# One order for TensorE with PSUM banks taken from a pool, and two feed-forward units moved behind attention

## The chip, the core and the metric

The kernel runs on one core of a Trainium2 chip. The metric is the device time of one execution in microseconds (us): the median of three runs was 1132.9 before the change (1132.64 to 1134.83). A difference of about 0.2% (2.3 us) is what a measurement of this kernel can tell from none.

The core has these engines: TensorE (PE, matrix products; its weight loads are shown as PEld), VectorE (DVE), ScalarE (ACT), GpSimd (POOL) and SyncE (SP, which here only issues DMAs). Each takes its instructions from a queue of its own, in order. Products land in PSUM, eight banks of 128 x 512 words; operands lie in SBUF. An engine waits for another by semaphores.

## The reference

For x of 2048 rows and 640 columns, attention a(x) with 32 heads of 20 columns and a gated feed-forward b(x) with 1728 features are mixed row by row by a gate. Attention works on four segments of 512 rows: within a segment it is causal softmax attention, and from the second segment on a memory M, z of the segments before it is read too.

```
def _A_ref(x, wq, wk, wv, wo, beta):          # H = 32, Dh = 20, N = 4, L = 512
    for s in range(N):
        logits = einsum("bhqd,bhkd->bhqk", qs, ks) * scale + mask
        a_dot = einsum("bhqk,bhkd->bhqd", softmax(logits), vs)
        a_mem = einsum(phi(qs), M) / (einsum(phi(qs), z) + 1e-6)
        o = g * a_mem + (1.0 - g) * a_dot      # g = sigmoid(beta), per head
        M, z = M + phi(ks)^T vs, z + sum(phi(ks))
    return o @ wo
def _B_ref(x, w1, w3, w2):
    return (silu(x @ w1) * (x @ w3)) @ w2
g = sigmoid((x * gate_w).sum(-1))
return g * a + (1 - g) * b
```

## The kernel before

**Numbers.** A product of two 32-bit operands is made of three passes over operands that are split into a high and a low part (`PASSES`): high by high, high by low, low by high. The split is an ACT copy into the rounded form and a subtraction on DVE or POOL (`split`, L487). `split_psum` (L518) does the same for operands of x and for the row maxima, but first copies the high part into a PSUM bank with ACT, so that the DVE subtraction has one input in SBUF and one in PSUM. It is called 10 times for x (segments 2 and 3, L687) and 32 times for the row maxima (L1210).

**Dense work.** The segments are taken in pairs, A = (0, 1) and B = (2, 3). For each pair: q, k and v projections (`proj`), the memory, then the feed-forward in five groups of features, `GROUPS` (L1417): [13, 0, 1], [2, 3, 4], [5, 6, 7], [8, 9, 10], [11, 12]. For most features a `unit` (L1023) makes the gate and up products of both segments with seven half products instead of eight: 54 matmuls of 128 x 512, tile names g, w, x (also under g) and u, four weight tiles from DRAM, and some twenty steps on DVE, ACT and POOL. `ffn_down` (L1127, tile f) multiplies a group by w2 and adds each of the five blocks of a segment into `acc` with one DVE step (L1149). `normalize(c)` (L1322) scales the attention output of segment c by the row sums (tile rr), adds the memory part (transposes, tile gt) and splits it; `oproj(c)` (L1390) multiplies by wo (tile op, 75 matmuls for each of two segments at the end), and `finish` writes the result.

**Attention.** It runs through 32 quads of four heads. A quad has two visits (`VISITS`, L1358), a big one of eight fills and a small one of three. An s fill makes scores in two banks, with four or two matmuls each, of which DVE takes the row maxima (L1200, sixteen per quad, each a pass over the bank and a short accumulator read). `max_rows` (L1206) brings the maxima back as two more rows of q by a DMA (qk<-mr). A t fill makes transposed scores less the maxima in two banks; ACT takes the exponential into P (L1232), POOL clears what the mask forbids (L1241). The o fill (`pv_quad`, L1246) multiplies P by v with a column of ones, which gives the row sums too, and stores the result to DRAM (od<-oq, L1258). After the last quad of a segment `o_sums` (L1265) loads its row sums back (rs<-od, L1267, on SP's queue), `o_scale` (L1274) takes their reciprocal on DVE, splits it in three (L1281 to L1286) and writes it out to be rR (L1288). `load_out` loads the attention output back, with the memory part on POOL's queue (L1316) and the rest on SP's (L1303, L1305).

**The order.** The program is traced once, with dense jobs fed between visits at a pace that spreads them (`segs`, each with an end in heads, and the main loop from L1582), and with a `tail` (L1514) behind the last visit. `braid(a, b, every)` puts a step of b behind each `every` steps of a. During tracing `bank_tile` (L496) gives each PSUM tile one of eight banks, by a small model of when banks come free; the choice is then fixed. At the end `Model.arrange` (L231) makes the final order of every queue by simulating all engines: `length` (L78) gives each instruction a time; each instruction has a due time, worked back from PE's order; every engine other than PE takes the ready instruction that is due first; PE takes, among the next `AHEAD` = 48 groups (up to three dense matmuls, or one fill), the first that is ready and whose banks are free:

```
for g in range(first, min(first + AHEAD, len(groups))):
    if g not in gone and not wants[g] and earlier[g] <= gone and all(map(enabled, groups[g])):
        run = groups[g][::-1]
```

The order found is then tied down with dependencies. On the chip each engine follows it, whatever the real times are.

Of the kernel before, what the change touches and what calls it, by code (L numbers as in the profile page):

```python
# [19 lines left out]
P = 128  # L20
# [12 lines left out]
LANES, SPARE, SOON = 8, 3, 5000  # L33
# [7 lines left out]
ON_CHIP = {}  # L41
ENGINES = {mybir.EngineType.PE: "PE", mybir.EngineType.DVE: "DVE", mybir.EngineType.Activation: "ACT",
# [6 lines left out]
class Tags:  # L49
# [28 lines left out]
def length(i, e, outs, ins):  # L78
# [9 lines left out]
    if e == "PE":  # L88
# [6 lines left out]
        else:  # L95
            d = 0.453 * n * (2 if wide and n < 500 else 1) + (20 if wide else 0)
        return d, max(d, 232) + 165
    if e == "DVE":
        d = 155 + 1.04 * n
        if "Transpose" in kind:  # L100
            d = 200
        elif "Reciprocal" in kind:
            d = 150 + 6.2 * n
        elif len(outs) > 1:
            d += 97
    elif e == "ACT":
        d = 170 + 0.85 * n
    else:
        d = 100 + (2.3 if len(ins) > 1 else 0.98) * n
# [3 lines left out]
class Model:  # L113


    def __init__(self, tc, nc, tags):
# [4 lines left out]
        self.end, self.free, self.gaps = [], {e: 0.0 for e in GAP}, {e: [] for e in GAP}  # L121
        self.lane, self.flown, self.way = [], {"HW": [], "SW": []}, 0.0

    def box(self, ap):
# [6 lines left out]
        if tag[0] == "b" and tag[1:].isdigit():  # L131
# [22 lines left out]
    def add(self, i):  # L154
# [8 lines left out]
        for write, args in ((False, ins), (True, outs)):  # L163
            for a in args:
# [4 lines left out]
                bank = not dram and box[1:] == (P, 0, 4 * L) and self.tags[name][0][0] == "b"  # L169
# [60 lines left out]

    def arrange(self):  # L231
# [11 lines left out]
        due, t = [math.inf] * n, 0.0  # L243
        for k in range(n):
            if eng[k] == "PE":
                due[k] = t
                t += dur[k]
        after, before = [[] for _ in range(n)], {}
        for x, (g, c) in tiles.items():
# [5 lines left out]
            if y is not None:  # L255
                before[users[x][0]] = users[y][0]
        for k in reversed(range(n)):
            if eng[k] != "PE":
                for s in succ[k] + after[k]:
                    due[k] = min(due[k], due[s] - HOP[eng[s]] - land[k])  # L260
                if k in before:
                    due[k] = min(due[k], due[before[k]])
        for k in range(n):
            if due[k] == math.inf:
                due[k] = t
        left = [len(p) for p in pred]
        ready = {e: [] for e in GAP}
        groups, group, earlier, tail = [], {}, [], {}
        for k in range(n):
# [12 lines left out]
            tail[x] = len(groups) - 1  # L282
        groups = [ks for _, ks in groups]
        wants = [sum(len(pred[k]) for k in ks) for ks in groups]
        gone, first, run = set(), 0, []
        busy = {e: 0.0 for e in GAP}
# [1384 lines left out]
```

## Time and profile before

| what | value |
|---|---|
| median of three runs | 1132.9 us |
| the profiled execution | 1130.5 us, span 1128.7 us |
| PE, DVE, POOL, ACT busy | 1096.7, 732.3, 510.2, 410.6 us |
| mean granted clock of PE | 0.991 of full |
| DMA | 222.8 MB moved, mean 197 GB/s |
| first and last matmul of attention starts | 129.9 us, 1054.1 us |

A row of the timeline has start and length in us, then engine, line, operation, output <- inputs, shapes and a count of merged instructions; in brackets the idle time before it and what ended it. A row of the waits has the total, the times and the longest. A matmul's length is its latency, and consecutive ones overlap, so its rate is read from starts. PE's busy time counts matmuls that stand within a run.

### The profile page before, as it was taken

To read this page: it belongs to the slowest core of one execution; us is meant where nothing else is said; L and a number is where in the kernel's file an instruction comes from. 1 tells how busy PE (TensorE), PEld (TensorE's weight loads), DVE (VectorE), ACT (ScalarE), POOL (GpSimd) and SP (SyncE) were. 2 spreads that over 40 slices of the span, in tenths; PEclk is the share of its full clock that TensorE was granted. 3 is DMA by queue.
4 is the path that set the end of the run, shared out by engine and by line. 5 is a ranking of instruction groups with operands and counts; after the bars stand their busy time and mean duration, and the time that the engine had idled before them with its cause. 6 is when DMAs were issued, how large, how long until landed. Compare 5 with 4: busy or idle time off the path is not lost.

```text
span 1128.7 us, 18096 instructions
## 1 busy us (share of the span) xinstructions
PE 1096.7 (97%) x6152; PEld 828.8 (73%) x6152; DVE 732.3 (65%) x1905; ACT 410.6 (36%) x825; POOL 510.2 (45%) x633
## 2 busy tenths in 40 slices
PE   9999999999999999899999998999999999999978
PEld 6988877767767777568877676767777667767756
DVE  6022568786886878884445577776776776775474
ACT  6244235232322323353344443334423423425110
POOL 6085334794875868646473213322322332322400
PEclk9999999999999999999999999999999999999979
DMA  8389745574755657976478776576756656634832
GB/s 300 133 257 313 266 147 163 194 251 151 228 186 175 214 170 225 292 221 190 154 246 265 246 228 186 155 230 206 193 142 181 184 137 179 182 113 154 258 99 84
DMA packets 120475, 222.81 MB, mean 197 GB/s; under 512 B 13280, under 2 KB 32896, under 8 KB 120384
## 3 DMA queue, kind: packets, MB, share of 16 engines
q1 hardware_dynamic: 95920, 175.91, 46.7%
q0 software_dynamic: 20432, 38.68, 15.1%
q10 hardware_dynamic: 4032, 7.08, 1.7%
q8 instruction: 49, 0.80, 0.3%
q14 instruction: 42, 0.34, 0.1%
HBM read 125.92 MB, written 94.78 MB: 196 GB/s over the span
## 4 chain that ended last, share of the span: by engine, by line
PE 51%; DMA 2%; DVE 2%; ACT 1%; issue 1%; SPq 0%; DVEq 0%; ACTq 0%
PE g L1033 8%; PE f L1141 7%; PE op L1404 6%; PE o L1252 4%; PE q L698 3%; PE u L1033 3%; PE s L1193 3%; PE v L828 3%; PE k L698 3%; PE t L1228 3%; PE w L1033 1%; PE g L698 1%; DMA od<-oq 1%; PE u L698 1%; PE nd L796 1%; ACT P L1232 1%
## 5 line engine op out<-in xcount | busy, mean ns | idle before, releaser
L1200 DVE CUSTOM_DVE_ANT_0 junk<-s,mask 128x256 bf16<-128x256 f32 (+3 forms) x512 | 250.8, 490 | 105.9 <-PE s L1193 69.4
L1232 ACT ACTIVATE P<-t 128x512 f32<-128x512 f32 x320 | 167.7, 605 | 160.2 <-PE t L1228 157.8
L1141 PE MATMUL f<-ht,W 128*128 128x512 f32 x820 | 203.6, 401 | 4.9 <-ACT ht L488 1.9
L1141 PEld LDWEIGHTS f<-ht,W 128*128 128x128 f32 x820 | 151.8, 189 | 45.5 <-POOL ht L489 2.5
L1241 POOL TENSOR_SCALAR_AFFINE_SELECT P<-P 128x512 f32<-128x512 f32 (+1 forms) x160 | 91.5, 581 | 157.0 <-ACT P L1232 154.5
L618 POOL TENSOR_TENSOR W<-wr,W 128x640 fp32r<-128x640 f32 (+3 forms) x92 | 139.9, 1521 | 6.9
L1170 POOL DMA_DIRECT2D qk<-qkd x128 | 83.0, 650 | 105.5 <-PE s L1193 53.6
L617 POOL CAST W<-wr 128x640 fp32r<-128x640 f32 (+3 forms) x92 | 71.5, 777 | 129.2 <-PE v L828 43.4
L489 POOL TENSOR_TENSOR ht<-fu,ht 128x512 fp32r<-128x512 f32 x44 | 58.6, 1337 | 73.6 <-ACT ht L488 73.6
L1193 PE MATMUL s<-qk 60*128 60x256 f32 (+3 forms) x512 | 79.9, 355 | 0.7 <-DVE oq L1256 0.3
L1404 PE MATMUL op<-N,W 128*128 128x512 f32 x300 | 77.9, 409 | 1.4 <-issue 0.6
L1252 PE MATMUL o<-P,vg 128*32 128x512 f32 (+3 forms) x1024 | 75.6, 435 | 1.7 <-DVE fw L1095 0.9
L1149 DVE TENSOR_TENSOR acc<-f,acc 128x512 f32<-128x512 f32 x80 | 54.5, 689 | 31.2 <-PE f L1141 30.5
L1033 PE MATMUL u<-T,W 128*128 128x512 f32 x264 | 70.3, 399 | 3.2 <-DVE fv L1075 3.2
L1033 PE MATMUL g<-XB,W 128*128 128x512 f32 x264 | 72.1, 401 | 0.1
L1228 PE MATMUL t<-qk 62*128 62x256 f32 (+3 forms) x512 | 69.1, 336 | 1.3 <-ACT P L1232 0.7
L1193 PEld LDWEIGHTS s<-qk 60*128 60x128 f32 x512 | 43.8, 186 | 34.9 <-issue 21.2
L1404 PEld LDWEIGHTS op<-N,W 128*128 128x128 f32 x300 | 55.7, 193 | 17.2 <-issue 1.9
L1228 PEld LDWEIGHTS t<-qk 62*128 62x128 f32 x512 | 46.3, 187 | 23.8 <-issue 11.4
L1252 PEld LDWEIGHTS o<-P,vg 128*32 128x32 f32 x1024 | 30.4, 109 | 45.1 <-issue 34.4
L1033 PEld LDWEIGHTS u<-T,W 128*128 128x128 f32 x264 | 48.7, 188 | 16.4 <-DVE fv L1075 4.5
L1033 PEld LDWEIGHTS g<-XB,W 128*128 128x128 f32 x264 | 48.3, 188 | 12.9 <-issue 0.4
(194 smaller groups left out, 1836.7 us busy)
## 6 DMA issues: line engine op xcount, KB each, us to landing
qk<-qkd POOLq DMA_DIRECT2D x128, 240.0 KB, 4.7
wr<-in_w_dram SPq DMA_DIRECT2D x40, 320.0 KB
qkd<-qs SPq DMA_DIRECT2D x20, 512.0 KB
qkd<-ks SPq DMA_DIRECT2D x20, 512.0 KB
wd_down<-W SPq DMA_DIRECT2D x14, 640.0 KB
W<-wd_down SPq DMA_DIRECT2D x14, 640.0 KB
od<-oq SPq DMA_DIRECT2D x32, 256.0 KB
wd_all<-W SPq DMA_DIRECT2D x11, 640.0 KB
```

The source lines that it names most:

```text
L618: nc.gpsimd.tensor_sub(w[:, 1, :n], src, w[:, 0, :n].bitcast(F32))
L698: nc.tensor.matmul(ps, w[:, a, kb * P:(kb + 1) * P], xs(c, b, kb), start=n == 0, stop=n == 14)
L1033: nc.tensor.matmul(ps, w[:, a, col + i * P:col + (i + 1) * P], x(i, b), start=start and t == 0, stop=stop and t == 3 * n - 1, skip_group_c ...
L1141: nc.tensor.matmul(ps[:, :n1 - n0], w, h, start=n == 0, stop=n == len(ms) - 1)
L1170: here(nc.gpsimd.dma_start(t[64 * i:64 * i + RH], qkd[c][RH * (h + i):RH * (h + i + 1)]))
L1193: nc.tensor.matmul(ps[i][:, o:o + w], q[:, qb * P:(qb + 1) * P], key[:, :w], start=n == 0, stop=n == len(todo) - 1, skip_group_check=True)
L1200: r = nc.vector.tensor_tensor_reduce(out=junk[:, :w], in0=ps[i][:, o:o + w], in1=mask[:, L - w:], scale=1.0, scalar=-3.0e38, op0=ALU.add, ...
L1228: nc.tensor.matmul(ps[i][:, o:o + L - kb * P], key[:, kb * P:(kb + 1) * P], q[:, kb * P:], start=n == 0, stop=n == len(todo) - 1, skip_gro ...
L1232: last["exp"] = nc.scalar.activation(pt[:, i], ps[i], AF.Exp, scale=SCALE)
L1241: nc.gpsimd.affine_select(d, d, pattern=pattern, base=0, channel_multiplier=-1, compare_op=ALU.is_ge, fill=0.0)
L1252: nc.tensor.matmul(ps[32 * i:32 * i + 32, kb * P:], heads[2 * p + i]["v"][:, kb], pt[:, i % 2, o:o + L - kb * P], start=kb == 0, stop=kb = ...
L1404: nc.tensor.matmul(ps, ws[kb][:, b, fb * P:(fb + 1) * P], n_tile(c, kb)[:, a], start=n == 0, stop=n == 14)
```

## The change

Four things.

**The order** is made by a new function `schedule`, which `arrange` calls for each of two settings of (stay, pause, spare, near) and takes the order that ends first by its own reckoning. PE's choice (`choose`) is new: within a visit it takes the next fill of the same visit that can go, and if one can go within `stay` (300 or 150 ns) it waits for it; else it takes the group that is first in turn, or waits for it if it can go within `pause` (150 ns); only then others. Leaving dense work for a visit is reckoned at `TURN` = 93 ns more, matmuls after a window of 3413 ns that was more than half idle at double length. A freed buffer, and a result for another engine, count 50 ns later than before.

**Banks.** All PSUM tiles are one tag of eight in the model; a tile gets a bank when the simulated PE reaches it, of those free the one whose last tile stands latest in program order, provided that tiles in a bank stay in program order (`seq`). A group out of turn must leave `RESERVE` = 4 banks that can still serve the earliest tile without one. The plan found is written in the string `BANKS`, one digit per tile, and the program is traced with it. `split_psum` no longer uses a bank or the ACT copy into it; its subtraction reads the high part from SBUF.

**Costs.** In `length` the 97 ns extra for a DVE instruction with two outputs (the row maxima) go; short 32-bit matmuls cost 3.4 instead of 2 times the base; POOL's affine select has its own cost; what waits for the load of the row sums (rs) is let go `LATE` = 2000 ns after its reckoned landing, so the DVE steps on the row sums are placed later.

**The tail.** The units of the last group of pair B, features 11 and 12, leave the last dense segment of the attention stage and stand behind the last visit, with the loads of segment 2's attention output between their steps; then the last `ffn_down` with the loads for segment 3 and `normalize(2)` between its steps; then the output projections as before.

```diff
-LANES, SPARE, SOON = 8, 3, 5000
+LANES, WINDOW, TURN, LATE, HANG = 8, 3413, 93, 2000, 0
+CHOICES, ROUNDS = ((300, 150, 3, 5000), (150, 150, 3, 5000)), 1
+RESERVE = 4
...
+BANKS = (
+    "0012310202020202020202001121101121101121101121101102120303032145671556742351572517175213461515643272"
...
-    def tile(self, shape, dt, name, tag=None, bufs=None):
+    def tile(self, shape, dt, name, tag=None, bufs=None, real=None):
         kw = {}
         if tag is not None:
-            kw["tag"] = tag
+            kw["tag"] = real or tag
         if bufs is not None:
-            kw["bufs"] = bufs
...
-            d = 0.453 * n * (2 if wide and n < 500 else 1) + (20 if wide else 0)
+            d = 0.453 * n * (3.4 if wide and n < 200 else 1) + (20 if wide else 0)
...
-        elif len(outs) > 1:
-            d += 97
...
-        d = 100 + (2.3 if len(ins) > 1 else 0.98) * n
+        d = 208 + 0.84 * n if "Affine" in kind else 100 + (2.3 if len(ins) > 1 else 1.0) * n
...
+    def schedule(self, plan, due, stay, pause, spare, near):
...
+        def fits(g):
+            new = [tiles[x][1] for k in groups[g] for x in set(of.get(k, ())) if users[x][0] == k and x not in held and tiles[x][0] == "bank"]
+            if not new:
+                return True
+            m, chosen = low(), set()
+            for i in new:
+                b = max((b for b in range(8) if not taken[b] and b not in chosen and seq[b] < i), key=lambda b: seq[b], default=None)
+                if b is None:
+                    return False
+                chosen.add(b)
+            if m in new:
+                return True
+            return sum(seq[b] < m and b not in chosen for b in range(8)) >= (1 if g == first else RESERVE)
+
+        def can(g):
+            return g not in gone and not wants[g] and earlier[g] <= gone and fits(g) and all(map(enabled, groups[g]))
+
+        def choose():
+
+            nonlocal first, of_late
+            while first in gone:
+                first += 1
+            if first == len(groups):
+                return None
+            if visit[of_late]:
+                for g in range(of_late + 1, len(groups)):
+                    if visit[g] != visit[of_late]:
+                        break
+                    if g not in gone:
+                        if can(g):
+                            return g
+                        if soon(g) <= now + stay:
+                            return None
+            if can(first):
+                return first
+            if soon(first) <= now + pause:
+                return None
+            for g in range(first + 1, min(first + AHEAD, len(groups))):
+                if can(g):
+                    return g
+            return None
...
+        def enabled(k):
+            if lane[k]:
+                some = LANES - (spare if due[k] + slip - now > near else 0)
+                if len(flown[lane[k]]) >= some and not landed.issuperset(flown[lane[k]][-LANES:1 - some or None]):
+                    return False
+            return all(x in held or eng[k] == "PE" and k != users[x][0] and group.get(users[x][0]) == group[k] or k == users[x][0] and (any(not taken[b] and seq[b] < tiles[x][1] for b in range(8)) if tiles[x][0] == "bank" else
+                       tiles[x][1] == given[tiles[x][0]] + 1 and room[tiles[x][0]] > 0)
+                       for x in of.get(k, ()))
...
+            if e == "PE":
+                w = int(now // WINDOW)
+                for q in range(int(since // WINDOW), w + 1):
+                    idle[q] = idle.get(q, 0) + max(0, min(now, (q + 1) * WINDOW) - max(since, q * WINDOW))
+                if idle.get(w - 1, 0) > WINDOW / 2:
+                    d *= 2
+                if visit[of_late] and not quick:
+                    d += TURN
+                quick = bool(visit[of_late])
+                since = now + d
...
+                    if tiles[x][0] == "bank":
+                        i = tiles[x][1]
+                        b = max((b for b in range(8) if not taken[b] and seq[b] < i), key=lambda b: seq[b])
+                        taken[b], seq[b], bankof[x] = 1, i, b
+                        got.add(i)
...
+            if lane[k]:
+                heapq.heappush(events, (done + HANG, serial + 2, n + k))
+                late = LATE if ops[k].outs[0].bass_ap.tensor.name.startswith("rs") else HANG
+                heapq.heappush(events, (done + late, serial + 3, 2 * n + k))
+            else:
+                heapq.heappush(events, (done + 50, serial + 2, n + k))
...
-                            for g in range(first, min(first + AHEAD, len(groups))):
-                                if g not in gone and not wants[g] and earlier[g] <= gone and all(map(enabled, groups[g])):
-                                    run = groups[g][::-1]
-                                    gone.add(g)
-                                    break
...
+        best, start = None, begin
+        for stay, pause, spare, near in CHOICES:
+            begin = start
+            for _ in range(ROUNDS):
+                due = wanted(begin)
+                found = self.schedule(plan, due, stay, pause, spare, near)
+                print("SCHEDULE", stay, pause, spare, near, found[0])
+                if best is None or found[0] < best[0]:
+                    best = found
+                begin = found[2]
+        _, order, when, flown, bankof = best
+        assert all(bankof[x] == int(b) for x, b in zip(self.banked, BANKS) if x in bankof), "the plan of the banks is an old one"
...
-        ps = pp.tile([P, L], F32, tag=f"b{k}", name=name, bufs=1)
+        ps = pp.tile([P, L], F32, tag="bank", name=name, bufs=NB, real=f"b{BANKS[len(model.banked)]}")
+        model.banked.append(ps.tensor.name)
...
 
     def split_psum(dst, src, name, pin=lambda ins: ins):
 
-        hi = bank_tile(name)[:, :src.shape[-1]]
-        pin(nc.scalar.copy(dst[:, 0], src))
-        nc.scalar.copy(hi, dst[:, 0].bitcast(F32))
-        nc.vector.tensor_sub(dst[:, 1], src, hi)
+        nc.scalar.copy(dst[:, 0], src)
+        nc.vector.tensor_sub(dst[:, 1], src, dst[:, 0].bitcast(F32))
...
     for g in (1, 2):
         seg += [job_down(B, g)] + units(B, g + 1)
-    seg += [job_down(B, 3)] + units(B, 4)
+    seg += [job_down(B, 3)]
     segs.append((NJ + LAG, seg))
+    un = chain(units(B, 4))
     dn = job_down(B, 4)
     plan = plan_wo()
     o1, o2 = jobs_oproj(2, plan, False)
     o3, o4 = jobs_oproj(3, plan)
-    tail = [(0, load_shares(B)), braid(dn, (0, chain2(load_out(2), o1[1])), 3)]
-    tail += [(0, load_out(3)), braid(o2, o3, 3, 6), o4]
+    tail = [(0, load_shares(B)), braid(un, (0, load_out(2)), 4)]
+    tail += [braid(dn, (0, chain2(load_out(3), o1[1])), 3), braid(o2, o3, 3, 6), o4]
 
```

More of the change, by code (lines that the diff above doesn't have):

```diff
@@ L130, in box @@
         tag, _, pitch = self.tags[name]
-        if tag[0] == "b" and tag[1:].isdigit():
+        if tag == "bank":
             return name, (0, P, 0, 4 * L)
@@ L168, in add @@
                 dram = name not in self.tags
-                bank = not dram and box[1:] == (P, 0, 4 * L) and self.tags[name][0][0] == "b"
+                bank = not dram and box[1:] == (P, 0, 4 * L) and self.tags[name][0] == "bank"
                 old = self.seen.setdefault(name, [])
@@ L254, in arrange @@
             y = slot.get((g, c + 1))
-            if y is not None:
+            if y is not None and g != "bank":
                 before[users[x][0]] = users[y][0]
[L257 to L267, printed above, removed]
+        of = {}
+        for x, u in users.items():
+            for k in u:
+                of.setdefault(k, []).append(x)
         groups, group, earlier, tail = [], {}, [], {}
@@ L282, in arrange @@
             tail[x] = len(groups) - 1
-        groups = [ks for _, ks in groups]
-        wants = [sum(len(pred[k]) for k in ks) for ks in groups]
-        gone, first, run = set(), 0, []
-        busy = {e: 0.0 for e in GAP}
-        given = {g: 0 for g in room}
-        use = {x: len(u) for x, u in users.items()}
-        of = {}
-        for x, u in users.items():
-            for k in u:
-                of.setdefault(k, []).append(x)
-        order = {e: [] for e in GAP}
-        when = [0.0] * n
@@ L311, in issue @@
-        def issue(e, k):
-            nonlocal serial
-            order[e].append(k)
-            when[k] = now
-            if lane[k]:
-                flown[lane[k]].append(k)
-            for x in of.get(k, ()):
-                if x not in held:
-                    held.add(x)
-                    given[tiles[x][0]] += 1
-                    room[tiles[x][0]] -= 1
-            busy[e] = now + dur[k] + GAP[e]
-            heapq.heappush(events, (busy[e], serial, -1))
-            done = now + land[k]
-            if lane[k]:
-                way[0] = max(way[0], now + dur[k] + QUEUE) + passage(ops[k])
-                done = way[0] + (FETCH if fetch(ops[k].ins) else POST)
-            heapq.heappush(events, (done, serial + 1, k))
-            serial += 2
@@ new lines, in arrange, with wanted @@
+        visit, v = [], 0
+        for g, (kind, _) in enumerate(groups):
+            name = kind[1]
+            quick = name[0] in "sto" and name[:2] != "op"
+            v += not quick
+            visit.append(v if quick else 0)
+        groups = [ks for _, ks in groups]
+        plan = groups, group, earlier, visit, of, succ, room
+        def wanted(begin):
+            due = [begin[k] if eng[k] == "PE" else math.inf for k in range(n)]
+            for k in reversed(range(n)):
+                if eng[k] != "PE":
+                    for s in succ[k] + after[k]:
+                        due[k] = min(due[k], due[s] - HOP[eng[s]] - land[k])
+                    if k in before:
+                        due[k] = min(due[k], due[before[k]])
+            last = max(begin)
+            return [min(d, last) for d in due]
```

203 lines of the change are left out of this document (142 added, 61 removed).

## The prediction

> **What bounds the kernel now.** I read the page first, then the waits of TensorE (PE), then the timeline and the chain of the last 75 us, then the visits to attention in PE's timeline.
>
> ```profile
> span 1128.7 us, 18096 instructions
> ...
> PE 1096.7 (97%) x6152; PEld 828.8 (73%) x6152; DVE 732.3 (65%) x1905; ACT 410.6 (36%) x825; POOL 510.2 (45%) x633
> ...
> PEclk9999999999999999999999999999999999999979
> ```
>
> PE bounds it: 97% busy, the others far below. A gain must come from idle PE (1128.7 - 1096.7 = 32 us), from PE at a lower clock (the 7 in the last slices but one), or from busy time that is waiting inside a run of matmuls, which the page counts as busy. The waits of PE (total, times, longest):
>
> ```profile
> PE rr L1328 <- DVE acc L1149: 5.6, 1, 5.6
> PE u L1033 <- DVE fv L1075: 3.2, 2, 2.0
> PE rr L1328 <- DMA rR<-rp: 2.9, 1, 2.9
> ```
>
> The longest single wait lies in the tail. PE's timeline there (start, length, idle before):
>
> ```profile
> 1056.49 13.34 PE L1141 MATMUL f<-ht,W 128*128 128x512 f32 x57
> ...
> 1076.83 0.58 PE L1328 MATMUL rr<-rR,sel 96*128 96x512 bf16 x1 [5.63 <-DVE acc L1149]
> ...
> 1080.51 0.59 PE L1328 MATMUL rr<-rR,sel 96*128 96x512 bf16 x1 [1.39 <-DVE on L1335]
> ...
> 1082.53 1.62 PE L1404 MATMUL op<-N,W 128*128 128x512 f32 x3 [0.58 <-issue]
> ...
> 1097.39 0.39 PE L1328 MATMUL rr<-rR,sel 96*128 96x512 bf16 x1
> 1097.62 0.60 PE L1334 MATMUL gt<-ident,N 128*128 128x128 f32 x4
> 1097.98 2.33 PE L1404 MATMUL op<-N,W 128*128 128x512 f32 x9
> ```
>
> VectorE (DVE) beside it, then the chain that ended last:
>
> ```profile
> 1067.79 0.69 DVE L1149 TENSOR_TENSOR acc<-f,acc 128x512 f32<-128x512 f32 x1 [0.69 <-PE f L1141]
> 1074.58 0.95 DVE L1281 RECIPROCAL rs<-rs 128x128 f32<-128x128 f32 x1 [6.10 <-DMA rs<-od]
> ...
> 1076.10 0.68 DVE L1149 TENSOR_TENSOR acc<-f,acc 128x512 f32<-128x512 f32 x1
> ...
> 1077.75 0.29 DVE L1286 TENSOR_TENSOR rR<-rs,rR 128x128 bf16<-128x128 f32 x1
> ```
>
> ```profile
> 1055.61 14.41 DMA od<-oq
> ...
> 1070.08 0.55 SPq L1267
> ...
> 1073.91 4.97 DMA N<-od
> ...
> 1103.77 20.22 PE op L1404 x87
> ```
>
> The last head's output takes 14.41 us to land. The load of the row sums (L1267) stands in SP's queue and waits for it, and loads of N stand behind it. DVE has the reciprocal at the head of its queue and sits idle 6.10 us; two evictions of f wait behind it although PE has finished their banks; so PE's rr gets no bank and idles 5.63 us. Then comes the clock:
>
> ```profile
> 1069.70:1073.40 3.70, 1.51 (x7) 0.77 (x7) 0.00 (x0) 0.00 (x0) 0.00 (x0) 1.00 0.44 136
> 1073.40:1087.10 13.70, 8.30 (x27) 6.38 (x27) 9.80 (x18) 1.85 (x3) 0.00 (x0) 0.50 0.51 165
> ```
>
> (Columns: length, busy time of PE, weight loads, DVE, ACT, POOL, then the granted clock.) For 13.7 us PE runs at 0.50.
>
> **The tail.** One full matmul costs 20.22 / 87 = 0.2324 us. From 1056.49 on, PE has 60 matmuls of f (13.9 us), 150 of op (34.9 us) and ten steps of rr with four transposes (1097.39 to 1097.98, 0.59 each, 5.9 us): 54.7 us, so it could end at 1111.2. It ends at 1103.77 + 20.22 = 1123.99. Lost: 12.8 us, of which 5.63 + 1.39 + 0.58 = 7.6 is idle and the rest, 5.2, the half clock. The change puts units 11 and 12 (2 x 54 matmuls, 25.1 us) behind the last o, ahead of the f of the last group. This is no work more or less; the same 25.1 us leave the attention stage. Behind the last o then lie 25.1 + 13.9 = 39.0 us of dense matmuls before op of segment 2 begins. The chain that they must hide, from 1055.61: landing at 1070.02, the reciprocal possible at 1074.58, the five short DVE steps behind it, the last (L1286) done at 1078.04, and one more transfer that I take at 5 us, as N<-od: 1083, about 28 us. Cover 39 us against 28, so the 12.8 us go, all but a remainder. The change also lets the plan count 2 us more for the landing of the row sums, so that the reciprocal is put behind DVE work that is ready; this takes the evictions from behind it. What moves along: eight weight loads of the two units now run beside the loads of N, and SP's queue still holds L1267 in order, so a wait there now holds back weights instead of N. Bounds: gain 6 (a stall of the old kind in half size) to 12.8; I take 11, since 39 against 28 us is not close.
>
> [...] The row has 13.7 us at half clock after 5.63 us of idle PE. [...]
>
> **The visits.** PE leaves dense work for stretches of s, t and o rows. In the timeline I count 116, from the first to the last:
>
> ```profile
> 129.93 0.98 PE L1193 MATMUL s<-qk 60*128 60x512 f32 x8
> ```
>
> ```profile
> 1052.02 2.36 PE L1252 MATMUL o<-P,vg 128*32 128x512 f32 x32
> ```
>
> Written are two per quad of four heads, 64; the 52 others are splits, where the next fill was not ready and the order took dense groups between. What a split costs, by the small visit in one piece and in two:
>
> ```profile
> 857.66 0.87 PE L1033 MATMUL w<-T,W 128*128 128x512 f32 x3
> 858.46 0.50 PE L1193 MATMUL s<-qk 60*128 60x256 f32 x4
> ...
> 859.42 0.96 PE L1033 MATMUL w<-T,W 128*128 128x512 f32 x3
> 860.22 1.56 PE L1033 MATMUL g<-T,W 128*128 128x512 f32 x6
> ```
>
> ```profile
> 978.79 0.87 PE L1033 MATMUL g<-XE,W 128*128 128x512 f32 x3
> 979.59 0.74 PE L1193 MATMUL s<-qk 60*128 60x256 f32 x8
> 980.26 1.66 PE L1033 MATMUL g<-XB,W 128*128 128x512 f32 x6
> 981.85 0.51 PE L1228 MATMUL t<-qk 62*128 62x384 f32 x4
> 982.28 0.96 PE L1033 MATMUL g<-XE,W 128*128 128x512 f32 x3
> 983.08 0.86 PE L1033 MATMUL g<-XB,W 128*128 128x512 f32 x3
> ```
>
> In one piece: 857.66 to 860.22 is 2.56 us, less six dense matmuls (1.39) makes 1.17. In two: 978.79 to 983.08 is 4.29, less twelve (2.79) makes 1.50. A split costs 0.33 us, 52 of them 17 us. The new order stays in a visit when the next fill comes within 300 ns (or 150: two plans are made and the shorter by its own reckoning is kept) and waits 150 ns for the group that is due. A merge so buys 0.33 us for a wait of 0 to 0.3, on average perhaps 0.15. Banks are now taken from one pool when the order is made instead of fixed beforehand, so a fill waits for any free bank and not for a certain one. If half of the splits go: 26 x (0.33 - 0.15) = 4.7 us; the pool's part has no row. Its upper bound is the rest of the 17, its lower bound below nothing, since a reserve of banks (four for a group out of turn) also forbids orders that were allowed. I take 3 for it: 8 us in all, bounds +6 (slower) to -17.
>
> **The rest.** Waits outside visits and tail (u for fv, 3.2; rr for rR, 2.9) come from DVE work placed in front of evictions and from a transfer that the plan saw earlier. New costs per instruction and the later row sums shift these; some go, others come. I take 2 us, bounds -6 to +4. `split_psum` loses a ScalarE copy and a bank each time, 42 times, and its subtraction now takes both inputs from SBUF. ACT at 36% of the span gives nothing for it. The subtraction:
>
> ```profile
> L1076 DVE TENSOR_TENSOR fv<-fv,fw 128x512 f32<-128x512 f32 x22 | 20.8, 947 | 0.5
> ...
> L1075 DVE TENSOR_TENSOR fv<-fv,u 128x512 f32<-128x512 f32 x22 | 15.1, 686 | 3.8 <-PE u L1033 3.1
> ```
>
> The same add with both inputs in SBUF takes 947 ns, with one from PSUM 686. For the ten full ones that is at most 2.6 us of DVE time, hidden by the same stage's PE work; uncovered it would be those 2.6 us. The 32 small ones (16 columns of 512) together make one full one, at most 0.3 us. [...]
>
> **The sum.** The profiled execution took 1130.5 us with a span of 1128.7; the median of the three runs, 1132.9, is 2.4 above it, and the differences are taken from the median. 11 + 8 + 2 = 21: 1112. Late is then PE itself.
>
> **Rivals.** (1) Only the tail gains: the visits stay split, since the fills wait for ACT and DVE to drain and not for a certain bank. Against: the small visit at 858.46 went in one piece. 1132.9 - 11 = 1122. (2) The cover fails: L1267 in SP's queue now holds back weights of unit 12 or of op. For: the 14.41 us landing. A stall as long as the one now (5.63) and half of the loss to the half clock (5.2) give back some 8 to 9 of the 11: 1121. (3) All works: the visits win 15 of their 17 us, the tail all 12.8, the rest 6: 1132.9 - 33.8 = 1099. Against: waits must replace nearly no split. (4) Slower: the plan counts each row maximum 97 ns cheaper than before and orders PE by that; PE is in order and stands at each s fill until DVE is done.
>
> ```profile
> 635.46 0.69 DVE L1200 CUSTOM_DVE_ANT_0 junk<-s,mask 128x512 bf16<-128x512 f32 x1
> ...
> 636.30 0.69 DVE L1200 CUSTOM_DVE_ANT_0 junk<-s,mask 128x512 bf16<-128x512 f32 x1
> ```
>
> A pair stands 0.84 us apart, the new plan says 0.155 + 1.04 x 0.512 + 0.014 = 0.70. With sixteen maxima per quad the plan misses up to 2.2 us of DVE; it decides against the gain when more than 21 / 32 = 0.66 us per quad reaches PE. At 1 us: 1112 + 32 = 1144. Against: last maxima of a fill give the next instruction a shorter start, narrower ones are nearer to the plan, and DVE has room even where visits are densest:
>
> ```profile
> 871.40:1054.30 182.90, 182.04 (x1072) 127.52 (x1071) 122.95 (x356) 68.67 (x136) 59.08 (x82) 1.00 0.57 163
> ```
>
> Here 122.95 of 182.90 is 67%. Less two units (nine DVE steps each, between the 0.69 and 0.95 of the rows above, some 14 us) and 25.1 us it is 109 of 158, 69%: moving the units doesn't make DVE the bound.
>
> **Chances.** Forecast 0.50 (its own range 1105 to 1119); (1) 0.17; (2) 0.08; (3) 0.12; (4) 0.09; gains and new waits that cancel, 0.04. Within 0.2% (2.3 us, about what a measurement of this kernel tells from no change) is that last case: 0.04. Slower is (4): 0.09. Faster is the rest, 0.87. The range 1098 to 1126 takes in the forecast, (1), (2) and most of (3), and leaves out some 0.18.
>
> **What would show it.** Tail: no idle over 1 us between the last o and the last op, clock 1.00 there, the reciprocal behind all ready evictions, about 39 us of g, u, w and f rows behind the last o. Visits: well under 116 stretches, 75 to 95, without long lone waits at s or t. Wrong would be: L1267 followed by weight loads and a stall of g, u or op for W; as many stretches as before; waits of s or t for DVE m or ACT P that sum to over 10 us.

## The result, and the profile after

The changed kernel takes 1124.2 us (median; 1119.6 to 1126.4) where the kernel before takes 1133.0 on the same chip: ratio 0.9921, 95% interval 0.99 to 0.9943. It is 8.8 us faster; forecast were 21. On another chip, later, it took 1124.8 (ratio 0.9939, 0.9918 to 0.9959). The profiled execution took 1123.65 us. Its page:

```profile
span 1121.9 us, 17966 instructions
...
PE 1098.2 (98%) x6152; PEld 820.2 (73%) x6152; DVE 729.0 (65%) x1905; ACT 399.9 (36%) x783; POOL 509.9 (45%) x633
...
PEclk9999999999999999999999999999999999989999
```

The 7 at the end of the clock's row is gone; an 8 has come three slices earlier (slice 36 of 40, 982 to 1010 us). The waits of PE (total, times, longest), the longest groups:

```profile
PE t L1376 <- DVE m L1348: 2.3, 3, 1.6
PE f L1289 <- DMA W<-wd_down: 2.1, 1, 2.1
```

No rr stands there any more, and gt only with 0.2 us. PE's timeline of the tail, from the f of the last group to the last op:

```profile
1059.71 13.39 PE L1289 MATMUL f<-ht,W 128*128 128x512 f32 x57
...
1076.70 0.66 PE L1482 MATMUL gt<-ident,N 128*128 128x128 f32 x4 [0.22 <-DVE on L1477]
...
1095.35 0.97 PE L1552 MATMUL op<-N,W 128*128 128x512 f32 x3 [0.55 <-DVE on L1483]
...
1096.75 20.40 PE L1552 MATMUL op<-N,W 128*128 128x512 f32 x87
```

DVE beside it, and the two stretches behind attention, the moved units and then the rest (length, then busy time of PE, weight loads, DVE, ACT, POOL, then the granted clock):

```profile
1044.87 0.95 DVE L1429 RECIPROCAL rs<-rs 128x128 f32<-128x128 f32 x1 [0.23 <-DMA rs<-od]
```

```profile
1034.58:1059.71 25.13, 25.13 (x109) 20.29 (x108) 12.25 (x21) 5.32 (x9) 7.54 (x9) 1.00 0.86 258
1059.71:1117.15 57.44, 56.51 (x261) 43.56 (x259) 38.71 (x59) 7.99 (x13) 6.43 (x5) 1.00 0.43 142
```

The reciprocal now waits 0.23 us instead of 6.10 and runs beside the units. From the start of f to the end of the last op are 57.4 us (1096.75 + 20.40 - 1059.71), against 67.5 before and 54.7 without any loss; the clock is at 1.00 in both stretches. So the tail gained 10.0. The units still stand ahead of this f, only behind attention instead of in it, so without a cost or a gain f would start at 1056.5 as before. It starts at 1059.7: ahead of the tail 3.2 us were lost, where a gain of 10 was forecast. The same stretch of attention, from the 24th o to the 32nd, before and after:

```profile
871.90:1052.00 180.10, 179.24 (x1039) 126.39 (x1037) 121.06 (x352) 67.71 (x135) 59.08 (x82) 1.00 0.56 161
```

```profile
865.70:1030.80 165.10, 162.89 (x955) 112.81 (x955) 113.93 (x343) 61.19 (x119) 53.40 (x77) 0.97 0.56 156
```

Not all of the 25.1 us left these eight quads, since the other dense work moved too: 84 matmuls fewer stand there (1039 to 955). By the timeline 77 of them are dense ones, 17.9 us at 0.2324, and the stretch became 15.0 us shorter, so it lost some 3. DVE's share is 113.93 of 165.10, 69%, as forecast. What goes wrong is in one place that the share doesn't show, and it holds nearly all of the stretch's 2.2 us of idle PE and its loss of clock (0.03 of 165.1 is 5 us, half of the 10.2 below). PE, then DVE, then the window around it and the one behind:

```profile
997.70 0.96 PE L1289 MATMUL f<-ht,W 128*128 128x512 f32 x3
998.59 0.74 PE L1341 MATMUL s<-qk 60*128 60x512 f32 x6
1000.89 1.22 PE L1376 MATMUL t<-qk 62*128 62x512 f32 x6 [1.57 <-DVE m L1348]
1002.36 0.80 PE L1376 MATMUL t<-qk 62*128 62x256 f32 x4 [0.24 <-DVE m L1348]
1003.40 1.65 PE L1289 MATMUL f<-ht,W 128*128 128x512 f32 x3 [0.24 <-DVE m L1348]
```

```profile
998.70 0.69 DVE L1297 TENSOR_TENSOR acc<-f,acc 128x512 f32<-128x512 f32 x1 [0.60 <-PE f L1289]
999.30 0.68 DVE L1348 CUSTOM_DVE_ANT_0 junk<-s,mask 128x512 bf16<-128x512 f32 x1
...
1000.14 0.69 DVE L1348 CUSTOM_DVE_ANT_0 junk<-s,mask 128x512 bf16<-128x512 f32 x1
1000.75 0.08 DVE L1348 DVE_READ_ACCUMULATOR2_ANT m<- 128x1 f32 x1
1000.87 0.69 DVE L1348 CUSTOM_DVE_ANT_0 junk<-s,mask 128x512 bf16<-128x512 f32 x1
```

```profile
998.70:1004.40 5.70, 3.65 (x18) 2.54 (x19) 5.12 (x17) 2.07 (x4) 1.38 (x3) 0.69 0.24 86
1000.90:1011.10 10.20, 9.71 (x35) 6.49 (x36) 4.85 (x19) 5.22 (x10) 2.76 (x5) 0.50 0.01 3
```

One eviction of f and eight maxima keep DVE busy for 5.12 of 5.70 us. The order gives PE only three matmuls of f at a time to put between (3 x 0.2324 = 0.7 us at full clock; each nine of them bring DVE another eviction of 0.69). PE waits until the second maximum is read, and then runs 10.2 us at half clock. Idle 1.57 + 0.24 + 0.24 and half of 10.2 make some 7 us. On the other chip the changed kernel loses its time at the same place (1.71 us of idle ahead of the t at 1003.85).

### The profile page after: what moved, and what is told of

It reads as the page before. It is cut to its first block, busy times and chain, and to the rows that moved or that the text cites. A ratio compares the mean times of both kernels' runs of the same rounds, so it can differ in the third digit from the quotient of the medians.

```text
span 1121.9 us, 17966 instructions
## 1 busy us (share of the span) xinstructions
PE 1098.2 (98%) x6152; PEld 820.2 (73%) x6152; DVE 729.0 (65%) x1905; ACT 399.9 (36%) x783; POOL 509.9 (45%) x633
## 4 chain that ended last, share of the span: by engine, by line
PE 61%; DVE 8%; DMA 4%; POOL 3%; issue 2%; ACT 1%; SPq 0%; ACTq 0%; DVEq 0%; POOLq 0%
PE f L1289 13%; PE g L1181 11%; PE o L1400 5%; PE s L1341 4%; PE u L1181 4%; PE op L1552 4%; PE t L1376 4%; PE q L846 3%; PE v L976 3%; PE k L846 3%; PE w L1181 2%; PE g L846 2%; DVE junk L1348 2%; DMA W<-wd_out 2%; PE u L846 1%
## 5 line engine op out<-in xcount | busy, mean ns | idle before, releaser
L1289 PE MATMUL f<-ht,W 128*128 128x512 f32 x820 | 208.4, 405 | 5.3 <-DMA W<-wd_down 2.1
L765 POOL CAST W<-wr 128x640 fp32r<-128x640 f32 (+3 forms) x92 | 68.1, 741 | 134.1 <-PE v L976 43.4
L1341 PE MATMUL s<-qk 60*128 60x256 f32 (+3 forms) x512 | 73.9, 355 | 2.1 <-DVE m L1348 0.8
L1376 PE MATMUL t<-qk 62*128 62x256 f32 (+3 forms) x512 | 66.1, 340 | 4.3 <-DVE m L1348 2.3
L1341 PEld LDWEIGHTS s<-qk 60*128 60x128 f32 x512 | 40.6, 187 | 38.8 <-issue 22.0
```

Source lines behind the costliest of these rows:

```text
L1289: nc.tensor.matmul(ps[:, :n1 - n0], w, h, start=n == 0, stop=n == len(ms) - 1)
L1341: nc.tensor.matmul(ps[i][:, o:o + w], q[:, qb * P:(qb + 1) * P], key[:, :w], start=n == 0, stop=n == len(todo) - 1, skip_group_check=True)
L1376: nc.tensor.matmul(ps[i][:, o:o + L - kb * P], key[:, kb * P:(kb + 1) * P], q[:, kb * P:], start=n == 0, stop=n == len(todo) - 1, skip_gro ...
```

## The experiments

My first theory was that the tail gains its ten microseconds and the new order, with more stretches of attention than before, costs what is missing. Its rival: the order costs nothing, and the two units are missed where they stood, as dense work behind which DVE's bursts were hidden. For each run I give the median and the ratio to the kernel before on the same chip with its interval; and from its profile the start of the last f ("f at") and the time from there to the end of the last op ("tail"), by the two rows that show them. "f at" is that of one execution: in a second profile of the changed kernel it is 1062.7, 3.0 us later, with the same tail (57.4); the difference arises ahead of the 24th o, which starts at 865.7 and at 868.6, and from there to the 32nd it takes 165.1 us both times. The kernel before has f at 1056.5 and a tail of 67.5, the changed one 1059.7 and 57.4.

**The tail's edit alone, in the kernel before.**

```diff
-    seg += [job_down(B, 3)] + units(B, 4)
+    seg += [job_down(B, 3)]
+    un = chain(units(B, 4))
-    tail = [(0, load_shares(B)), braid(dn, (0, chain2(load_out(2), o1[1])), 3)]
-    tail += [(0, load_out(3)), braid(o2, o3, 3, 6), o4]
+    tail = [(0, load_shares(B)), braid(un, (0, load_out(2)), 4)]
+    tail += [braid(dn, (0, chain2(load_out(3), o1[1])), 3), braid(o2, o3, 3, 6), o4]
```

> The kernel before with one edit: units 11 and 12 and the loads placed behind the end of attention as in the change, all else (order, banks, costs, split_psum) as before. Theory (the tail carries the gain by itself, the new order gives nothing or takes a little): 1133 - 10 = 1123 us, last idle of PE in the tail under 1 us and clock 1.00 there; 126 stretches of attention are in its order. Rival (the tail needs the new order, above all the 2 us on the row sums): the reciprocal still stands in front of evictions, a stall of 3 us or more and a half clock stay, 1127 us or more.

Measured: 1130.4, ratio 0.999 (0.997 to 1.0009). No change. Its timeline and its longest wait:

```profile
1067.92 13.36 PE L1141 MATMUL f<-ht,W 128*128 128x512 f32 x57
...
1103.64 20.45 PE L1404 MATMUL op<-N,W 128*128 128x512 f32 x87
```

```profile
PE u L1033 <- DVE fv L1075: 6.8, 4, 2.6
```

The tail takes 56.2, 11.3 less; f starts 11.4 later. The whole gain is given back ahead of the tail, with the old rule for the order in the kernel: this speaks for the rival. Not all of it is lost within attention, though. Of the four waits of u for DVE one stands behind the last o (1035.57), among the moved units:

```profile
1051.62 2.91 PE L1033 MATMUL u<-T,W 128*128 128x512 f32 x6 [2.31 <-DVE fv L1075]
```

With 3.4 us at half clock behind it (1051.7 to 1055.1), this is some 4 of the 11.4.

**The other half: all of the change but the tail's edit.** The lines above, the other way round, in the changed kernel.

> The changed kernel with the tail of before (units 11 and 12 back in the attention stage), banks planned anew. Theory: the new order by itself loses about what it lost ahead of the tail in the changed kernel, 3 us: 1134 to 1138 us, 142 stretches of attention in its order. Rival (the order gains, and something in the tail lost it again): under 1130 us.

Measured: 1124.7, ratio 0.9948 (0.9931 to 0.9965).

```profile
1051.10 13.41 PE L1289 MATMUL f<-ht,W 128*128 128x512 f32 x57
1070.93 1.75 PE L1482 MATMUL gt<-ident,N 128*128 128x128 f32 x7 [4.62 <-DVE acc L1297]
1075.86 1.97 PE L1482 MATMUL gt<-ident,N 128*128 128x128 f32 x8 [3.17 <-DVE on L1483]
...
1097.65 20.40 PE L1552 MATMUL op<-N,W 128*128 128x512 f32 x87
```

f starts 5.4 us earlier than before; the tail (66.95) keeps its stall and its half clock, so the 2 us more that the plan counts for the row sums don't mend it. The order gains by itself, so the first theory falls, and the rival takes its place from here on. Putting the tail's edit on top of the order moves f by +8.6 (1051.1 to 1059.7) and the tail by -9.5; by the ratios (0.9948, then 0.9921 and 0.9939) 1 to 3 us are left of it. These were measured on different chips and their intervals overlap, so a net gain of the tail's edit on top of the new order is not shown.

**Why the visits stay split.** In the changed kernel I count 143 stretches of attention, in the kernel before 116. Without both waits of the plan:

```diff
-CHOICES, ROUNDS = ((300, 150, 3, 5000), (150, 150, 3, 5000)), 1
+CHOICES, ROUNDS = ((0, 0, 3, 5000),), 1
```

> The changed kernel with stay = 0 and pause = 0 (PE never waits for a fill or for the group in turn), banks planned anew. Theory: the wait for a fill was hardly ever used, because a fill that lacks a bank counts as never coming; the order has 143 stretches as with the wait, so the time stays within 3 us of the changed kernel (1121 to 1127). Rival (the waits cost what the order should have gained): 1118 us or less.

Measured: 1124.8, ratio 0.9949 (0.9929 to 0.997), and again 143 stretches. The rule that should merge visits does nothing, and the code says why: `soon` returns infinity as soon as `fits` finds no bank, so a fill that lacks a bank is never waited for, whatever `stay` is. With one setting (300, 150) and a `soon` that instead gives the time at which a taken bank comes free:

```diff
                         if tiles[x][0] == "bank":
-                            if not fits(g):
-                                return math.inf
+                            t = max(t, freed(g))
                             continue
```

> The changed kernel, but the reckoning of when a fill can go also looks at when a taken bank will be free, so that PE waits up to 300 ns for a bank too (pause 150 as in the change); banks planned anew; 120 stretches of attention in its order instead of 143. Theory: 23 splits fewer at 0.33 us each less about 0.15 of waiting: 4 us less than the changed kernel, 1118 to 1122 us. Rival (the fills wait for ACT and DVE to drain, so that a split avoided is a wait of the same length): 1123 to 1126 us.

Measured: 1126.1, ratio 0.9959 (0.9947 to 0.9971), with 120 stretches: 23 fewer, and no gain. By the pages, of one execution each, PE is busy for 3.5 us less than without waits (1098.3 to 1094.8) and idle for 7.0 us more (24.8 to 31.8): what the avoided splits save comes back as waiting.

**What in the order gains.** The new order with the old costs of `length`, and the tail of before:

```diff
-            d = 0.453 * n * (3.4 if wide and n < 200 else 1) + (20 if wide else 0)
+            d = 0.453 * n * (2 if wide and n < 500 else 1) + (20 if wide else 0)
...
+        elif len(outs) > 1:
+            d += 97
...
-        d = 208 + 0.84 * n if "Affine" in kind else 100 + (2.3 if len(ins) > 1 else 1.0) * n
+        d = 100 + (2.3 if len(ins) > 1 else 0.98) * n
```

> The kernel of e2 (new order, tail of before), but the costs per instruction of the kernel before; banks planned anew; 156 stretches of attention in its order against 142. Theory (what the new order gains over before, 6 us, comes from stalls that the new costs foresee): 1129 to 1133 us. Rival (it comes from the pool of banks and the new choice, whatever the costs): 1123 to 1127 us.

Measured: 1130.0, ratio 0.9989 (0.9969 to 1.0008). And the new costs alone, put into the kernel before:

> The kernel before with nothing but the changed costs of length() (an fp32r pass of under 200 columns, no 97 ns for the second output, the affine select): old pools of banks, old split, old tail, 111 stretches of attention. Theory (most of the order's 5 to 6 us ahead of the tail comes from the costs, since with the old costs the new order gained next to nothing): 1126 to 1129 beside 1132. Rival (costs and pools are worth something only together): 1131 to 1134.

Measured: 1127.1, ratio 0.9962 (0.9947 to 0.9978). Last, the new order with the old `split_psum` (a copy in a bank, the subtraction from PSUM) and the tail of before:

> New costs and new pools of banks, with the row sums split through a PSUM bank as before (the subtraction reads PSUM, the copy there is pinned) and the old tail; 143 stretches. Theory (the split of the row sums is off the path): as with the new split, 1124 to 1127. Rival (the split's bank and the pin were what held the fills): 1129 to 1133.

Measured: 1126.5, ratio 0.995 (0.9931 to 0.9969), against 0.9948 with the new one. So of the order's 6 us (0.0052 x 1132), the costs bring 4 to 5 (0.0038 alone; 0.0041 is what their loss takes away), the pool of banks what is left, 1 to 2 (0.0011 without the costs), the new split nothing that can be measured. Each of these has an interval of some 2 us to both sides, and they come from three chips. (This split is that of the row maxima and of x, not of the row sums, which the expectation names.) On DVE the new split does cost something. Its 32 small subtractions, with the new split and then with the old one:

```profile
L671 DVE TENSOR_TENSOR ns<-m,ns 128x16 fp32r<-128x16 f32 x32 | 11.3, 352 | 3.1 <-ACT ns L670 3.1
L674 DVE TENSOR_TENSOR ns<-m,nh 128x16 fp32r<-128x16 f32 x32 | 5.2, 163 | 5.9 <-ACT nh L673 5.9
```

With both inputs in SBUF the longest takes 1334 ns (in the changed kernel), with one in PSUM 172 (in the kernel before). The longest (313.70 to 315.03 in the changed kernel) ends with a POOL subtraction that reads SBUF too (313.43 to 315.00), and so does the next (379.92 to 381.18 beside 379.51 to 381.16). Eight of the 32 take 584 ns or more there, and each of them ends 0.03 to 0.04 us behind a POOL instruction that ran when it started; the 24 others take 176 ns or less. With the tail of before DVE is busy for 731.3 us by the page, with the old split for 723.1.

**Half of the move.** Unit 11 back in the attention stage, unit 12 behind it:

```diff
-    seg += [job_down(B, 3)]
+    seg += [job_down(B, 3), job_unit(B, 11)]
...
-    un = chain(units(B, 4))
+    un = job_unit(B, 12)
```

> The changed kernel with unit 11 back in the attention stage and only unit 12 behind it; banks planned anew. Theory (each unit taken out of the last eight quads costs there about what it gives in the tail, because DVE works in bursts that the dense matmuls had covered): half of the stretch's 5 to 9 us comes back, and the cover behind the last o falls to 12.6 + 13.9 = 26.5 us against a chain of about 28, a stall of 0 to 2: 1119 to 1123 us where the changed kernel takes 1124. Rival (the last stretch loses for another reason): 1124 us or more, since only cover is lost.

Measured: 1127.2, ratio 0.9958 (0.9934 to 0.9981), above the 1119 to 1123 of the theory.

```profile
1056.75 13.40 PE L1289 MATMUL f<-ht,W 128*128 128x512 f32 x57
...
1074.88 0.38 PE L1476 MATMUL rr<-rR,sel 96*128 96x512 bf16 x1 [1.77 <-DVE on L1477]
...
1084.82 0.38 PE L1476 MATMUL rr<-rR,sel 96*128 96x512 bf16 x1 [0.90 <-DMA rR<-rR]
...
1099.00 20.41 PE L1552 MATMUL op<-N,W 128*128 128x512 f32 x87
```

rr waits again in the tail, which takes 62.7: one unit is not enough cover. Against the new order with the tail of before, one unit moved costs 5.7 us ahead of f (1051.1 to 1056.75) and gains 4.3 in the tail; the second costs 3.0 more and gains 5.2. Both are missed where they stood.

**DVE made lighter.** Each row maximum is taken over the second half of its columns only and leaves out the first half; all else is as in the changed kernel. Once so, and once with the tail of before:

```diff
-                r = nc.vector.tensor_tensor_reduce(out=junk[:, :w], in0=ps[i][:, o:o + w], in1=mask[:, L - w:],
+                r = nc.vector.tensor_tensor_reduce(out=junk[:, :w // 2], in0=ps[i][:, o + w // 2:o + w], in1=mask[:, L - w // 2:],
```

> The changed kernel with the row maxima taken over the second half of each piece of scores only (left out: the first half of the columns of each maximum, so DVE has about 85 us less to do; the softmax is the same for any maximum that is near). Banks planned anew. Theory (DVE's bursts hold PE in the leaner last stretch): against the next kernel, which has the same relief but the tail of before, it is 7 to 11 us faster, as the tail alone gives. Rival (ACT, POOL, a transfer or the clock holds PE there): it is 3 us faster or less, as without relief.

> The kernel of e2 (new order, tail of before) with the same maxima over half of each piece (left out: the other half). Theory: 7 to 11 us slower than e6; loss ahead of the last o 4 to 8 us less than in e2. Rival: within 3 us of e6.

Measured: 1116.9, ratio 0.9869 (0.9841 to 0.9897), with both units moved; 1126.8, ratio 0.9958 (0.9936 to 0.9979), with the tail of before. The timelines:

```profile
1055.04 13.39 PE L1289 MATMUL f<-ht,W 128*128 128x512 f32 x57
...
1092.05 20.41 PE L1552 MATMUL op<-N,W 128*128 128x512 f32 x87
```

```profile
1051.43 13.39 PE L1289 MATMUL f<-ht,W 128*128 128x512 f32 x57
...
1079.07 1.97 PE L1482 MATMUL gt<-ident,N 128*128 128x128 f32 x8 [8.57 <-DVE on L1483]
...
1101.12 20.42 PE L1552 MATMUL op<-N,W 128*128 128x512 f32 x87
```

With the old tail the relief of DVE (731.3 to 659.7 us busy by the pages) brings nothing: f at 1051.4 against 1051.1. With the units moved it brings 4.7 us ahead of f (1059.7 to 1055.0): the move now costs 3.6 there instead of 8.6, and the tail gains 12.7 (70.1 to 57.4; its stall had become longer). That is what the theory says: DVE's work costs time where the dense filler is missing. By the medians the move gains 9.9 us here (1126.8 to 1116.9), where it gained 1 to 3 without the relief.

**A relief that keeps the computation.** The copies of the o banks go to ACT, 32 that take 0.69 us each on DVE; beside it the changed kernel again, on the same chip:

```diff
-        nc.vector.tensor_copy(ot, ps)
+        nc.scalar.copy(ot, ps)
```

> The changed kernel with the 32 copies of the o banks on ACT instead of DVE: 22.1 us (32 x 0.69 us) leave DVE. Theory (DVE's bursts hold PE where the dense filler was taken out): with the maxima over half of the columns about 110 us left DVE and 7 us came off the time, so in proportion some 1.5 us here, up to 3 because the copies of the last eight quads stand right where the stalls are: 1121 to 1123 against 1124. Rival (ACT is as tight there: its exps then wait behind the copies, and the banks of t and o come free later): 1125 to 1130.

> The changed kernel once more, beside the others on one chip. Theory: it keeps within the spread that it showed, 1120 to 1126 us. If its median comes out below 1121 or above 1127, the differences of 2 to 5 us between the variants measured on other chips can't be read.

Measured: 1117.3, ratio 0.9867 (0.9844 to 0.9891), against 1124.8, ratio 0.9939 (0.9918 to 0.9959). This beats both kernels, by 15 and by 7.5 us, far more than 22 us of DVE's 729 let me expect, also by the 70.6 us that the half maxima took off DVE (729.0 - 658.4 by the pages; the expectation reckons with 110). Its stretch from the 24th to the 32nd o, and its tail:

```profile
853.00:1021.40 168.40, 167.91 (x993) 116.53 (x989) 113.34 (x339) 68.14 (x131) 54.02 (x77) 1.00 0.57 163
```

```profile
1052.36 13.39 PE L1289 MATMUL f<-ht,W 128*128 128x512 f32 x57
...
1089.38 20.42 PE L1552 MATMUL op<-N,W 128*128 128x512 f32 x87
```

The stretch is 3.3 us longer than in the changed kernel, with 38 matmuls more in it (993 to 955). DVE's share there is 67% (113.34 of 168.40) instead of 69%, and PE idles 0.5 us instead of 2.2 and keeps its clock. The tail is 57.4 as in the changed kernel; all 7.3 us lie ahead of f. Whether they belong to the missing filler or are to be had anywhere, three more kernels tell: the same line with the tail of before, in the kernel before, and in the kernel before with the tail's edit.

> The new order with the tail of before, and the copies of the o banks on ACT. Theory (DVE's bursts cost time only where the dense filler was taken out; here the filler is still there): little in the attention stage, f of the last group at 1049 to 1052 against 1051.1 without this edit, and the tail still loses 10 to 13, so 1122 to 1125 against 1124.7. Rival (the copy on ACT is worth its 7 us anywhere and says nothing of the filler): 1117 to 1119.

> The kernel before with the copies of the o banks on ACT and nothing else. Theory: as with the new order, little without the tail edit: 1129 to 1132 against 1132. Rival (worth its 7 us anywhere): 1124 to 1126.

> The kernel before with the edit of the tail and the copies of the o banks on ACT; old order. Without the copies it took 1130.4, since the attention stage gave back 11.4 us of the tail's 11.5. Theory: the copies on ACT take half or more of that back, 1122 to 1125. Rival (what is given back has nothing to do with where the copy stands): 1128 to 1131 if the copy is worth nothing here.

Measured, in this order: 1121.8, ratio 0.9912 (0.9893 to 0.9931); 1125.9, ratio 0.9948 (0.9929 to 0.9967); 1133.2, ratio 1.0014 (0.9998 to 1.003). Their timelines:

```profile
1048.45 13.39 PE L1289 MATMUL f<-ht,W 128*128 128x512 f32 x57
...
1096.34 20.40 PE L1552 MATMUL op<-N,W 128*128 128x512 f32 x87
```

```profile
1051.06 13.34 PE L1141 MATMUL f<-ht,W 128*128 128x512 f32 x57
...
1099.00 20.40 PE L1404 MATMUL op<-N,W 128*128 128x512 f32 x87
```

```profile
1072.36 13.42 PE L1141 MATMUL f<-ht,W 128*128 128x512 f32 x57
...
1108.13 20.43 PE L1404 MATMUL op<-N,W 128*128 128x512 f32 x87
```

Here my theory half fell. The copy on ACT is worth 4 us with the tail of before in the new order (0.9948 to 0.9912) and 6 in the old, so a good part of its gain has nothing to do with the missing filler. In the kernel before with the tail's edit it gains nothing: there the move costs more with the copies on ACT, not less. All five pairs, with and without the tail's edit:

| kernel that the edit is put on | f at | tail | ratio to the kernel before |
|---|---|---|---|
| before | +11.4 | -11.3 | 1 to 0.999 |
| new order | +8.6 | -9.5 | 0.9948 to 0.9921 and 0.9939 |
| new order, half maxima | +3.6 | -12.7 | 0.9958 to 0.9869 |
| new order, copy on ACT | +3.9 | -10.9 | 0.9912 to 0.9867 |
| before, copy on ACT | +21.3 | -12.1 | 0.9948 to 1.0014 |

For the last eight quads alone I took from PE's timeline what the matmuls there would need at their best durations; the loss beyond that grows with the move by 8.3, 5.4, 3.1, 1.5 and 5.4 us, in the order of the table. It grows in each pair, and less wherever DVE is lighter. From the last o to f there are 32.4, 28.9, 30.1, 31.0 and 31.0 us; the changed kernel's 28.9 has no loss in it, so 1 to 4 us of the four others' f column arise among the moved units and not in attention. By the ratios, less what the tail gained, the move costs some 10, 6 to 9, 3, 6 and 20 us ahead of f, which agrees with the f column within some 2 us. In the last pair 13.1 of the 21.3 us arise ahead of the 24th quad, among them an rr of an earlier segment:

```profile
706.40 0.59 PE L1328 MATMUL rr<-rR,sel 96*128 96x512 bf16 x1 [4.23 <-issue]
```

The list from which the order is made ends earlier without the units, and PE's order differs from the fifteenth quad on, in this pair as in the four others. Why it fell out so badly in this one kernel is not settled. Nor is a rival to the finer comparisons: no run takes the filler out of one fixed order, so a part of each cost may be the luck of the order that was found.

## Why the prediction was wrong in part

**The tail: right.** Forecast -11 within 6 to 12.8, measured -10.0 in the profiles, and -9.5 to -12.7 in all five pairs. The reciprocal runs behind ready evictions, no idle there exceeds 0.55 us, and the clock stays at 1.00. SP's queue holding back weights, rival (2), did not come about: the moved units' stretch has PE busy for 25.13 of 25.13 us.

**The failed step: "the same 25.1 us leave the attention stage".** I took the units out of it at no cost, on the ground that moving them "doesn't make DVE the bound", since 69% of the stage would be DVE's. The share was right to the percent, and the step was wrong: a mean over 158 us says nothing of 5 us in which DVE has an eviction and eight maxima to do and PE waits for them. The move's price ahead of f was 11.4 on the old order and 8.6 on the new one, near the whole gain of the tail; 8.3 and 5.4 of it lie in the last eight quads. I named the work that hides the landing of the last output, and not the work that the units had been hiding.

**The visits: the mechanism was wrong.** Of -8 none came as I had it: not 26 splits fewer but 27 stretches more, because a fill that lacks a bank is not waited for, which stood in the new `soon`. And what I took a merge to buy (0.33 for a wait of 0.15) isn't there: with 23 stretches fewer the time stayed, and PE's idle time grew by 7.0 us. Rival (1) had named this cause, that fills wait for ACT and DVE to drain; its 1122 lies nearest to the result, but by other terms, since it had no loss of cover and no gain of the order. Yet the new order starts f 5.4 us earlier and is 6 us faster in the median, where visits and rest together were put at 10. It is mostly the new costs per instruction that bring it, which I had counted among the rest, at 2; that the order came to more than half of the 10 is luck. The split, put at no more than 2.6 + 0.3 us of DVE, took 8.2 (723.1 to 731.3), above all in the 32 small subtractions; in time nothing of it can be measured.

**Rival (4): not seen.** The maxima are 0.84 us apart and then 0.73 (999.30, 1000.14, 1000.87) where the plan has 0.70, but the waits of t for the maxima sum to 2.3 us, and taking the 97 ns out is part of the costs that gain. Its place was right: it is at the maxima that PE stands. Of what was held against this rival, the shorter start behind the last maximum shows in the kernel before: with other work of DVE behind it that work starts 0.62 us after a maximum of 512 columns, another maximum 0.84 us after it (medians, over starts with less than 0.25 us of idle DVE between). That narrower ones are nearer to the plan shows only in part: 384 columns take 0.60 where the plan has 0.57, 128 with another maximum behind them 0.44 where it has 0.30.

By profiles the sum is: order -5.4, cover +8.6, tail -10.0, together -6.8, and the spans differ by 1128.7 - 1121.9 = 6.8. In the medians it is 8.8. Against the forecast of 21 the profiles so miss 14: 8.6 by the cover, some 4.6 by the visits and the rest (5.4 for 10), 1 by the tail.

## What to carry to other kernels

Before dense work is moved to where it hides a wait, look up what it hides where it stands, in windows of a few microseconds and by the instructions that one visit queues on each engine; the mean share of a stage can be right and say nothing. A cover that is taken away may be made up by taking a burst's work to an engine that idles there: here one line, the o copies on ACT (busy for 61.19 of 165.10 us in the changed kernel's last eight quads), brought 7 us more to the changed kernel, and it had to be measured with and without the change to know what it belongs to. A planner's rule helps only if the case that it is for can reach it; run the rule switched off.

## What the runs showed of the hardware

The time at half clock did not follow the length of the stall at its start. After 1.57 us of idle PE the clock stood at 0.50 for 10.2 us (1000.90 to 1011.10), with PE busy for 9.71 of them. In the tail of the kernel before, with its stall of 5.63 us, it was 13.7 us (1073.40 to 1087.10). In the kernel with the tail's edit alone there is, behind an idle of 2.64 us, one stretch of 3.4 us at half clock, and then 1.00:

```profile
1000.55 2.92 PE L1033 MATMUL u<-T,W 128*128 128x512 f32 x6 [2.64 <-DVE fv L1075]
```

```profile
1000.50:1003.90 3.40, 3.35 (x8) 2.67 (x9) 2.86 (x8) 0.11 (x1) 0.00 (x0) 0.50 0.39 98
1003.90:1007.00 3.10, 2.66 (x26) 1.09 (x28) 2.41 (x6) 0.51 (x1) 1.27 (x1) 1.00 0.54 144
```

So a stall of 1.6 us cost 7 us in one place and one of 2.6 us some 4 in another. What sets the length the rows don't say: PE counts as busy for 9.71 of 10.20 us in the long case and for 3.35 of 3.40 in the short one, so its busy share doesn't tell them apart. The plan's own reckoning of the clock, in windows of one fixed length (`WINDOW`), is not tested by any run; what the rows show are these three lengths.
